# Attention scores of the later head pairs from 64x32 tiles over two banks, on queries without zeros

## The chip, the core and the metric

The kernel runs on one core of a Trainium2 chip. The core has TensorE (PE, whose weight loads are listed apart as PEld), VectorE (DVE), ScalarE (ACT), GpSimd (POOL) and SyncE (SP), which issues the DMA transfers here. The metric is the device time of one execution in microseconds (us), taken as the median of several runs. A profile is one further execution; it has a span (first to last instruction of the program) and a time of its own.

## The reference

Eight batches of eight heads, 576 positions, 64 dimensions per head. Heads 0 to 3 see the last 32 positions, heads 4 to 7 every fourth of the last 128. The result of attention goes through a gate with three matrices.

```python
scores = scale * np.matmul(q, k.transpose(0, 1, 3, 2))        # scale = 1/sqrt(64)
mask_plain = (rel >= 0) & (rel < window)                       # window = 32
mask_dil = (rel >= 0) & (rel < window * dilation) & (rel % dilation == 0)   # dilation = 4
scores = np.where(masks[None, :, :, :], scores, -1000000000.0)
attn = np.exp(scores - np.max(scores, axis=-1, keepdims=True))
attn = attn / (np.sum(attn, axis=-1, keepdims=True) + 1e-09)
x = np.matmul(attn, v)                                         # heads side by side: (8, 576, 512)
theta = x @ w_theta
zr, zi = x * np.cos(theta), x * np.sin(theta)
y = np.einsum('ts,bsd->btd', w_tok_r, zr) + np.einsum('ts,bsd->btd', w_tok_i, zi)
u = x + y
out = u + np.maximum(u @ w_ch, 0.0)
```

## The kernel before

**Attention.** The host sorts the positions of heads 4 to 7 by their remainder mod 4, so that each of their queries, too, needs only a band of keys. Heads go in pairs, four pairs in a batch (`NP = 4`), and queries in blocks of 32 (`QB`), 18 of them in a head (`2 * NJ`, `NJ = 9`). A block of 32 queries needs the 64 keys (`BW`) that end with its own. For a pair, the host lays the two heads' transposed queries one above the other on the 128 partitions, the 64 dimensions of the first on partitions 0 to 63 and those of the second on 64 to 127, and gives each block 64 columns: 32 for the first head with zeros on the lower half, 32 for the second with zeros on the upper half. One matmul with 128 rows and 64 columns of such a block (the weights) then streams 64 columns of keys and gives the scores of both heads (L614). Two blocks stand side by side in the partitions of a PSUM bank (`e` = 0, 1), five such double blocks in the pair's first bank `s`, four in its second. All are fp32; a profile has two records, and two weight loads, for each fp32 matmul.

**From scores to values.** VectorE adds the mask and takes the minimum into `P` and `mx` (L553), which frees the bank. ScalarE takes the exponentials (L649, three double blocks in one planned piece), VectorE their sums and reciprocals (L652, L653), GpSimd scales (L655). VectorE transposes 32x32 squares of `P` into `pt` in eight instructions (L673), and TensorE multiplies by the values (`o`, L773, 18 matmuls of 128 rows and 64 columns). ScalarE copies `o` out to `x` (L733) and rounds it to `xh` (L747), and the rest of `x` is taken by VectorE or GpSimd (L751, L753).

**The gate.** `th` (L842 to L849) is the product with `w_theta` in three fp32r matmuls of high and low parts each; the sine and cosine follow. In batches 0 and 1 the token product `y` (L1444) and in all batches the channel product `c` (L1477) are fp32r matmuls of 128x128 weights with 288 columns. From batch 2 on (`FIRST`) the token product is built from products `A`, `B`, `C` and `D` (L1235). VectorE adds `y` to `x` (L1418) and finishes `c` (L1453); ScalarE and GpSimd split sums into high and low parts (`u`: L481, L489, L1251, L1253).

**What sets the order.** All is recorded by a planner (`Order`): generators yield an engine and an estimated duration, and the planner lets the one with the lowest rank go first whose engine is free in its own reckoning. The instructions then stand in that order in each engine's queue. From the steady part on (`steady`), TensorE's order is written out by `phase`: while batch b goes through its token product, the scores of pairs 2 and 3 of batch b + 1 and of pairs 0 and 1 of batch b + 2 stand between its steps (`S_FAST`), and so do the value products of batch b + 1 (`PV_FAST`); the third figure that `phase` yields with each piece is the time for which it is entered in the plan, from which the ranks of the other engines' work (`due`) come. So a change of these figures moves rows of VectorE, ScalarE, GpSimd and SP, while TensorE keeps its order. Queries and keys are loaded two pairs ahead (`load_qk`, L322 and L324), values by `load_va` (L336).

## Time and profile before

| | |
|---|---|
| median of 3 runs | 557.34 us (555.86 to 557.61) |
| profiled execution | 555.45 us, span 553.7 us |
| granted clock of TensorE, mean | 0.994 |
| busy share: PE, PEld, DVE, ACT, POOL | 95%, 86%, 79%, 67%, 59% |
| scores of later pairs (L614, `s<-k,q`) | 1008 records in 28 pairs, 36.6 us busy |
| value products (L773, all) | 1152 records in 32 pairs |
| DMA | 124.42 MB, mean 225 GB/s |

The page gives busy time by engine, the span in 40 slices, the chain of work that ended last, the costliest groups of instructions and the DMA issues. In a row of a group or of the timeline, `s<-k,q 128*64 128x64 f32 x36` is a matmul that writes tile `s` from `k` and `q`, with weights of 128 rows and 64 columns, an output of 64 columns, and 36 records. A matmul's end is modelled; its start is measured. In the chain each piece begins where the piece ahead of it released it. A row of the view of waits has who waited, for whom, the sum in us, how often, and the longest.

### The profile page before, as it was taken

To read this page: it belongs to the slowest core of one execution; us is meant where nothing else is said; L and a number is where in the kernel's file an instruction comes from. 1 tells how busy PE (TensorE), PEld (TensorE's weight loads), DVE (VectorE), ACT (ScalarE), POOL (GpSimd) and SP (SyncE) were. 2 spreads that over 40 slices of the span, in tenths; PEclk is the share of its full clock that TensorE was granted. 3 is DMA by queue.
4 is the path that set the end of the run, shared out by engine and by line. 5 is a ranking of instruction groups with operands and counts; after the bars stand their busy time and mean duration, and the time that the engine had idled before them with its cause. 6 is when DMAs were issued, how large, how long until landed. Compare 5 with 4: busy or idle time off the path is not lost.

```text
span 553.7 us, 14354 instructions
## 1 busy us (share of the span) xinstructions
PE 528.7 (95%) x5296; PEld 478.8 (86%) x5296; DVE 435.5 (79%) x1359; ACT 373.1 (67%) x1029; POOL 329.4 (59%) x347
## 2 busy tenths in 40 slices
PE   5798898999999999999999999999999999999997
PEld 4643887888899899989999899989999899989997
DVE  3878897995588797989799988989799978848322
ACT  1589977858928478768775786768776777467320
POOL 1327868899774175655468375646468365817660
PEclk9999799999999999999999999999999999999999
DMA  8985245633578938994599828993698727680722
GB/s 297 400 332 186 99 139 202 222 144 119 165 256 265 343 155 283 341 282 173 189 326 306 299 86 274 363 281 118 236 325 282 277 90 219 209 274 28 233 85 86
DMA packets 59127, 124.42 MB, mean 225 GB/s; under 512 B 5424, under 2 KB 24624, under 8 KB 58800
## 3 DMA queue, kind: packets, MB, share of 16 engines
q1 hardware_dynamic: 59056, 123.49, 65.1%
q8 instruction: 42, 0.69, 0.5%
q14 instruction: 29, 0.24, 0.1%
HBM read 99.88 MB, written 23.59 MB: 223 GB/s over the span
## 4 chain that ended last, share of the span: by engine, by line
PE 65%; DVE 10%; DMA 9%; ACT 7%; POOL 5%; issue 2%; SPq 1%; POOLq 0%; ACTq 0%; DVEq 0%
PE c L1477 15%; PE th L842 11%; PE C L1235 8%; PE A L1235 7%; PE D L1235 6%; PE o L773 5%; PE B L1235 4%; PE s L614 4%; DVE pt L673 4%; DMA va<-in_vw_dram 3%; PE y L1444 2%; PE th L824 2%; DMA xn<-xd 1%; DMA st_wtk<-in_wtk_dram 1%; DMA q<-in_qT_dram 1%
## 5 line engine op out<-in xcount | busy, mean ns | idle before, releaser
L673 DVE STREAM_TRANSPOSE pt<-P 32x288 f32<-32x288 f32 x224 | 105.1, 469 | 13.1 <-POOL P L655 8.8
L1477 PE MATMUL c<-u,late_wc 128*128 128x288 f32 x768 | 109.1, 296 | 1.2 <-DVE x L1453 1.0
L1477 PEld LDWEIGHTS c<-u,late_wc 128*128 128x128 f32 x768 | 105.5, 188 | 4.7 <-DVE x L1453 1.5
L649 ACT ACTIVATE P<-P,mx 128x64 f32<-128x64 f32 x252 | 84.4, 337 | 2.9 <-DVE mx L553 2.6
L842 PE MATMUL th<-wthh,xh 128*128 128x512 f32 x224 | 75.0, 395 | 0.2 <-DVE K L1377 0.2
L655 POOL TENSOR_TENSOR P<-P,mx 128x576 f32<-128x576 f32 x32 | 38.2, 1192 | 57.6 <-DVE mx L653 50.4
L553 DVE CUSTOM_DVE_ANT_0 P<-s,mskb 128x64 f32<-128x64 f32 x252 | 39.0, 218 | 18.0 <-PE s L614 17.7
L1251 ACT CAST u<-x 128x288 fp32r<-128x288 f32 x48 | 20.6, 430 | 45.3 <-DVE x L1261 44.8
L842 PEld LDWEIGHTS th<-wthh,xh 128*128 128x128 f32 x224 | 42.0, 188 | 9.6 <-DVE K L1377 0.4
L1253 POOL TENSOR_TENSOR u<-x,u 128x288 fp32r<-128x288 f32 x48 | 41.6, 872 | 14.4 <-ACT u L1251 14.0
L649 ACT ACTIVATION_READ_ACCUMULATOR P<-P,mx 128x1 f32 x252 | 47.3, 188 | 0.0
L842 PE MATMUL th<-wthl,xh 128*128 128x512 f32 x112 | 44.4, 396 | 0.0
L733 ACT COPY x<-o 128x576 f32<-128x576 f32 x32 | 29.4, 920 | 19.6 <-PE o L773 19.5
L489 POOL TENSOR_TENSOR zl<-g,zh 128x512 fp32r<-128x512 f32 x7 | 9.1, 1298 | 53.5 <-ACT zh L481 53.5
L614 PE MATMUL s<-k,q 128*64 128x64 f32 x1008 | 36.6, 225 | 2.7 <-DVE K L1377 2.2
L614 PEld LDWEIGHTS s<-k,q 128*64 128x64 f32 x1008 | 32.8, 139 | 7.1 <-issue 2.7
L1453 DVE SCALAR_TENSOR_TENSOR x<-c,x 128x288 f32<-128x288 f32 x64 | 28.4, 451 | 11.6 <-PE c L1477 11.4
L773 PEld LDWEIGHTS o<-pt,va 128*64 128x64 f32 x600 | 20.4, 137 | 11.7 <-DVE pt L673 3.2
L773 PE MATMUL o<-pt,va 128*64 128x64 f32 x600 | 24.8, 227 | 5.8 <-DVE pt L673 2.9
L1015 POOL TENSOR_TENSOR s<-f,x 128x256 f32<-128x256 f32 x24 | 17.8, 740 | 12.2 <-DVE f L1003 10.0
L842 PEld LDWEIGHTS th<-wthl,xh 128*128 128x128 f32 x112 | 21.0, 188 | 4.2
L1095 POOL TENSOR_TENSOR s1l<-s,s1h 128x512 fp32r<-128x512 f32 x12 | 15.4, 1288 | 14.0 <-ACT s1h L1092 14.0
(232 smaller groups left out, 1576.3 us busy)
## 6 DMA issues: line engine op xcount, KB each, us to landing
q<-in_qT_dram SPq DMA_DIRECT2D x32, 576.0 KB, 6.0
late_wt_a<-tw_t SPq DMA_DIRECT2D x24, 576.0 KB, 6.8
wt_g<-tw_b SPq DMA_DIRECT2D x22, 576.0 KB, 6.4
va<-in_vw_dram SPq DMA_DIRECT2D x30, 320.0 KB, 4.9
k<-in_kT_dram SPq DMA_DIRECT2D x28, 304.0 KB, 6.2
out_dram<-x SPq DMA_DIRECT2D x28, 288.0 KB, 2.1
vb<-in_vw_dram SPq DMA_DIRECT2D x29, 256.0 KB, 4.5
xd<-xq SPq DMA_DIRECT2D x24, 288.0 KB, 5.3
```

The costliest lines, as they stand in the source:

```text
L553: pin(nc.vector.tensor_tensor_reduce(out=P[:, n], in0=ps[:, n - g0], in1=mskb[:, mask_of(pr, n)], op0=ALU.add, op1=ALU.min, scale=-SCALE, ...
L614: pe(nc.tensor.matmul(ps[64 * e:64 * e + 64, n - g0], q[:, qb], k[:, QB * qb:QB * qb + BW], start=not masked, stop=not masked or n == g1 - 1))
L649: table(nc.scalar.activation(P[:, n], P[:, n], AF.Exp, bias=mx[:, n:n + 1], scale=-1.0, accum_out=sm[:, n, :1]))
L655: pin(nc.gpsimd.tensor_tensor(P, P, mx.unsqueeze(2).to_broadcast([128, NJ, BW]), op=ALU.mult))
L673: pin(nc.vector.transpose(pmats[b, pr][k0:k0 + QB, :, hh, QB * e:QB * e + QB], P[p0:p0 + QB, :, QB * o:QB * o + QB]))
L733: pin(nc.scalar.copy(dst, src))
L773: pe(nc.tensor.matmul(ps[64 * hh:64 * hh + 64, BW * j:BW * j + BW], v[:, 64 * hh:64 * hh + 64], pmats[b, pr][:, j, hh], start=True, stop=T ...
L842: pe(nc.tensor.matmul(pt, l, r, start=(n == 0), stop=(n == 3 * NC - 1)))
L1235: pe(nc.tensor.matmul(ps, l, r, start=first and n == 1, stop=last and n == 3 * len(ks), skip_group_check=more))
L1253: pin(nc.gpsimd.tensor_tensor(ul[b, d][:, ts], x[:, ts], uh[b, d][:, ts].bitcast(F32), op=ALU.subtract))
L1453: pin(nc.vector.scalar_tensor_tensor(out=x[:, ts], in0=ps, scalar=0.0, in1=x[:, ts], op0=ALU.max, op1=ALU.add))
L1477: pe(nc.tensor.matmul(ps, l[:, cs], r[:, ts], start=(n == 0), stop=(n == 3 * NC - 1)))
```

## The change

It concerns the pairs from the third of batch 2 on (`EIGHT = 2 * NP + 2`, counted from 0: pairs 10 to 31, 22 of them). Their queries come without the zeros: 32 columns to a block, the first head on partitions 0 to 63 and the second on 64 to 127, half as many bytes. Each matmul of 128 rows and 64 columns becomes two of 64 rows and 32 columns, one for each head. There are eight places in the array for weights of this size, two by rows and four by columns, and the new function `eight` walks over all of them in turn: head 0's scores go to the first and third quarter of a bank's partitions and head 1's to the second and fourth, as before. For the first ten blocks, in the pair's first bank ("near"), head 0 stands on the lower 64 rows and head 1 on the upper; for the last eight, in the second bank ("far"), the host swaps the two heads' halves of `q` and `k` (`k` gets 32 more columns, since the two parts overlap). So the eight matmuls of four blocks, two near and two far, have eight different places, and no quarter of a bank is written from both row halves. `P`, the masks and everything behind are as before.

Also, `eight` takes both banks before its first matmul, and gives both to VectorE at its end, where each bank was taken and given by itself; the planner reckons 830 ns for a block (`SC_NS`) instead of 148 for each double block, and `phase` enters it for 0.85 instead of 1.35.

```diff
+JS = 5
+EIGHT = 2 * NP + 2
+KW = S + 32
...
+SC_NS = 830
...
         q = ap.tile([128, 2 * NJ, 2 * QB], F32, tag="q", name=f"q{b}_{pr}")
-        k = ap.tile([128, S + 32], F32, tag="k", name=f"k{b}_{pr}")
-        yield "DMA", dma(2 * S)
-        pin(nc.sync.dma_start(q, qT[b, pr]))
-        yield "DMA", dma(S + 32)
-        pin(nc.sync.dma_start(k, kT[b, pr]))
+        k = ap.tile([128, KW + QB], F32, tag="k", name=f"k{b}_{pr}")
+        if n < EIGHT:
+            yield "DMA", dma(2 * S)
+            pin(nc.sync.dma_start(q, q0[n]))
+        else:
+            q = q.rearrange("p a b -> p (a b)")[:, :S].rearrange("p (a b) -> p a b", b=QB)
+            yield "DMA", dma(S)
+            pin(nc.sync.dma_start(q, qT[n - EIGHT]))
+        w = KW if n < EIGHT else KW + QB
+        yield "DMA", dma(w)
+        pin(nc.sync.dma_start(k[:, :w], kT[b, pr][:, :w]))
...
+    def eight(b, pr, q, k, P, mx, held):
+        groups = ((0, JS), (JS, NJ))
+        for g0, g1 in groups:
+            ps, rel = yield from bank("s", f"s{b}_{pr}_{g0}")
+            held[g0] = ps[:, :(g1 - g0) * BW].rearrange("p (a b) -> p a b", b=BW), rel
+        yield "PE", SC_NS
+        for i in range(2 * NJ):
+            qb = i // 4 * 2 + i % 2 + 2 * JS * (i // 2 % 2)
+            if i >= 2 * 2 * (NJ - JS):
+                qb = 2 * JS - 2 + i % 2
+            n, e, far = qb // 2, qb % 2, int(qb >= 2 * JS)
+            for r in range(2):
+                rs, to = slice(64 * r, 64 * r + 64), QB * (2 * e + (1 - r if far else r))
+                pe(nc.tensor.matmul(held[JS * far][0][to:to + QB, n - JS * far], q[rs, qb],
+                                    k[rs, QB * (qb + far):QB * (qb + far) + BW], start=True, stop=True))
+        for g0, g1 in groups:
+            go(mask_scores(*held[g0], P, mx, pr, g0, g1, ("mask", b, pr, g0)))
...
-        for g0, g1 in ((0, 5), (5, NJ)):
+        if b * NP + pr >= EIGHT:
+            yield from eight(b, pr, q, k, P, mx, held)
+        for g0, g1 in ((0, 5), (5, NJ)) if not held else ():
...
-                        yield ("sc", c, q), scores(c, q), 1.35
+                        yield ("sc", c, q), scores(c, q), 1.35 if c * NP + q < EIGHT else .85
...
+    q0 = qT.reshape(B * NP, 128, 2 * NJ, 2 * QB)[:EIGHT]
+    near, far = 2 * JS, QB * 2 * JS
+    qh = qh.reshape(B * NP, 2, D, 2 * NJ, QB)[EIGHT:]
+    qT = np.concatenate([qh[:, :, :, :near], qh[:, ::-1, :, near:]], axis=3).reshape(-1, 128, 2 * NJ, QB)
+    kT = np.concatenate([kp[..., :far + QB], kp[:, ::-1, :, far:]], axis=3)
```

TensorE's order, in the first period that runs with `A` to `D`, at the scores of pair 3 of batch 3, behind the value product of pair 0. Before (`s_3_0` and `s_3_5` are the pair's two banks):

```order
L773 MATMUL o_0_2794<-pt_116,va_0_2154 64x64 x10
L773 MATMUL o_0_2794<-pt_116,vb_0_2267 64x64 x8
L614 MATMUL s_3_0_2815<-k_3_2297,q_3_2296 64x64 x10
L614 MATMUL s_3_5_2834<-k_3_2297,q_3_2296 64x64 x8
L1235 MATMUL B_0_2844<-wtkh_544,i1h_2460 128x288
```

Now:

```order
L803 MATMUL o_0_2880<-pt_116,va_0_2185 64x64 x10
L803 MATMUL o_0_2880<-pt_116,vb_0_2317 64x64 x8
L608 MATMUL s_3_0_2905<-k_3_2361,q_3_2360 32x64 x4
L608 MATMUL s_3_5_2906<-k_3_2361,q_3_2360 32x64 x4
L608 MATMUL s_3_0_2905<-k_3_2361,q_3_2360 32x64 x4
L608 MATMUL s_3_5_2906<-k_3_2361,q_3_2360 32x64 x4
L608 MATMUL s_3_0_2905<-k_3_2361,q_3_2360 32x64 x4
L608 MATMUL s_3_5_2906<-k_3_2361,q_3_2360 32x64 x4
L608 MATMUL s_3_0_2905<-k_3_2361,q_3_2360 32x64 x4
L608 MATMUL s_3_5_2906<-k_3_2361,q_3_2360 32x64 x4
L608 MATMUL s_3_0_2905<-k_3_2361,q_3_2360 32x64 x4
L1265 MATMUL B_0_2948<-wtkh_544,i1h_2528 128x288
```

The block stays where it was, with 36 matmuls for 18, four to one bank and four to the other in turn. No other row of TensorE moves.

VectorE's order in batch 1, while the `P` of batch 2's pairs 2 and 3 are transposed into `pt` and the last three `y` of the first half of the positions are added. Before:

```order
L753 TENSOR_TENSOR xh_0_1928<-x_0_1880,xh_0_1928 128x512
L673 STREAM_TRANSPOSE pt_116<-P_2_1798 32x9x32 x3
L1418 TENSOR_TENSOR x_1_1013<-y_1_0_1937,x_1_1013 128x288
L673 STREAM_TRANSPOSE pt_116<-P_2_1798 32x9x32
...
L478 CAST u_2_2079<-x_2_1188 128x288
L673 STREAM_TRANSPOSE pt_118<-P_3_1901 32x9x32 x4
L751 TENSOR_TENSOR xh_1_2036<-x_1_1997,xh_1_2036 128x64
L753 TENSOR_TENSOR xh_1_2036<-x_1_1997,xh_1_2036 128x512
L1418 TENSOR_TENSOR x_3_1342<-y_3_0_2078,x_3_1342 128x288
```

Now:

```order
L703 STREAM_TRANSPOSE pt_116<-P_2_1798 32x9x32
L1448 TENSOR_TENSOR x_1_1013<-y_1_0_1968,x_1_1013 128x288
L703 STREAM_TRANSPOSE pt_116<-P_2_1798 32x9x32 x3
...
L488 CAST u_2_2112<-x_2_1188 128x288
L703 STREAM_TRANSPOSE pt_118<-P_3_1918 32x9x32 x5
L1448 TENSOR_TENSOR x_3_1342<-y_3_0_2111,x_3_1342 128x288
L703 STREAM_TRANSPOSE pt_118<-P_3_1918 32x9x32
L783 TENSOR_TENSOR xh_0_1973<-x_0_1896,xh_0_1973 128x512
L781 TENSOR_TENSOR xh_1_2079<-x_1_2028,xh_1_2079 128x64
L783 TENSOR_TENSOR xh_1_2079<-x_1_2028,xh_1_2079 128x512
```

The sum with the fourth `y` (`y_3`) now stands ahead of the last transpose and of three `xh`, one of which stood ahead of all transposes.

SP's order in the same period as the first example, from the weights for `D` to the output of batch 2. Before:

```order
L1117 DMA wt_g<-tw_b_2489 128x1152 x2
L322 DMA q_2_3056<-in_qT_dram 128x1152
L324 DMA k_2_3057<-in_kT_dram 128x608
L336 DMA va_0_3025<-in_vw_dram 128x640
L354 DMA vb_0_3189<-in_vw_dram 128x512
L322 DMA q_3_3222<-in_qT_dram 128x1152
L908 DMA xd_3228<-xq_2851 32x18x128 x4
L1117 DMA wt_g<-tw_b_2468 128x1152 x2
L915 DMA xn_3334<-xd_3228 64x512
L915 DMA xn_3334<-xd_3228 128x512 x4
L324 DMA k_3_3223<-in_kT_dram 128x608
L336 DMA va_1_3188<-in_vw_dram 128x640
```

Now:

```order
L1147 DMA wt_g<-tw_b_2556 128x1152
L331 DMA q_2_3178<-in_qT_dram 128x576
L1147 DMA wt_g<-tw_b_2556 128x1152
L334 DMA k_2_3179<-in_kT_dram 128x640
L346 DMA va_0_3134<-in_vw_dram 128x640
L364 DMA vb_0_3316<-in_vw_dram 128x512
L346 DMA va_1_3315<-in_vw_dram 128x640
L938 DMA xd_3377<-xq_2951 32x18x128 x4
L1147 DMA wt_g<-tw_b_2533 128x1152 x2
L945 DMA xn_3459<-xd_3377 64x512
L945 DMA xn_3459<-xd_3377 128x512 x4
L331 DMA q_3_3359<-in_qT_dram 128x576
```

`va_1` moved ahead of `xd` and `xn`, `q_3` behind both, and the second half of the weights behind `q_2`.

More of the change, by code (lines that the diff above doesn't have):

```diff
@@ L249, in build @@
 @with_exitstack
-def build(ctx, tc, qT, kT, vw, wth, wtk, wch, maskb, ident, identb, outT):
+def build(ctx, tc, q0, qT, kT, vw, wth, wtk, wch, maskb, ident, identb, outT):
     nc = tc.nc
@@ L407, in first_loads @@
             yield "DMA", dma(2 * S)
-            pin(nc.sync.dma_start(q, qT[0, pr]))
+            pin(nc.sync.dma_start(q, q0[pr]))
             yield "DMA", dma(KE)
-            pin(nc.sync.dma_start(k, kT[0, pr]))
+            pin(nc.sync.dma_start(k, kT[0, pr][:, :KE]))
             qks[0, pr] = (q, k, None)
@@ L1667, in build @@
     steady()
-_INS = ["qT", "kT", "vw", "wth", "wtk", "wch", "maskb", "ident", "identb"]
+_INS = ["q0", "qT", "kT", "vw", "wth", "wtk", "wch", "maskb", "ident", "identb"]
 def _arrays(inp):
@@ L1687, in _arrays @@
         qT[:, :, hh, :, :, hh] = qh[:, :, hh]
-    qT = qT.reshape(B, NP, 128, 2 * NJ, 2 * QB)
-    kT = np.zeros((B, NP, 128, S + 32), k.dtype)
-    kT[..., 32:] = k.transpose(0, 1, 3, 2).reshape(B, NP, 128, S)
+    q0 = qT.reshape(B * NP, 128, 2 * NJ, 2 * QB)[:EIGHT]
+    kp = np.zeros((B * NP, 2, D, KW), k.dtype)
+    kp[..., 32:] = k.transpose(0, 1, 3, 2).reshape(B * NP, 2, D, S)
+    near, far = 2 * JS, QB * 2 * JS
+    qh = qh.reshape(B * NP, 2, D, 2 * NJ, QB)[EIGHT:]
+    qT = np.concatenate([qh[:, :, :, :near], qh[:, ::-1, :, near:]], axis=3).reshape(-1, 128, 2 * NJ, QB)
+    kT = np.concatenate([kp[..., :far + QB], kp[:, ::-1, :, far:]], axis=3)
+    kT[:EIGHT, ..., :KW] = kp[:EIGHT]
+    kT = kT.reshape(B, NP, 128, KW + QB)
     vp = np.zeros((B, H, S + 32, D), v.dtype)
@@ L1713, in _arrays @@
     identb = np.where(ident > 0, 0x3F80, 0).astype(np.uint16)
-    return dict(qT=qT, kT=kT, vw=vw, wth=wth, wtk=wtk, wch=wch, maskb=maskb, ident=ident, identb=identb)
+    return dict(q0=q0, qT=qT, kT=kT, vw=vw, wth=wth, wtk=wtk, wch=wch, maskb=maskb, ident=ident, identb=identb)
 def kernel(**inputs):
```

## The prediction

> **What bounds the kernel now.** I read the page's busy shares first, then the busy times by window of the repeating part, then the chain of waits in order of time, then who waited for whom on TensorE.
>
> ```profile
> span 553.7 us, 14354 instructions
> ...
> PE 528.7 (95%) x5296; PEld 478.8 (86%) x5296; DVE 435.5 (79%) x1359; ACT 373.1 (67%) x1029; POOL 329.4 (59%) x347
> ```
>
> TensorE is busy 95% of the span. An average says little, so the next view takes one of the periods in which a batch runs (there are four of them from 206 us on, each with four of the changed score blocks).
>
> ```profile
> core 0: us, PE busy (x) PEld busy (x) DVE busy (x) ACT busy (x) POOL busy (x), PEclk, DMA share, GB/s
> 206.00:267.40 61.40, 61.40 (x634) 57.49 (x636) 55.02 (x183) 45.47 (x136) 37.40 (x41) 1.00 0.76 256
> ```
>
> In this period of 61.40 us TensorE is busy for 61.40 at a granted clock of 1.00, and the next engine, VectorE, for 55.02. The chain of waits there is TensorE's own work, piece after piece (columns: start, length, what):
>
> ```profile
> 205.99 1.20 PE s L614 x36
> 207.19 2.58 PE A L1235 x18
> 209.77 1.20 PE o L773 x36
> 210.97 1.05 PE s L614 x36
> ```
>
> So a score block is on the path with its whole length: 36 records, two for each of its 18 fp32 matmuls. It takes 1.05 us when the value block `o` stands ahead of it, which uses the same tile shape, and 1.20 when a 128-row, 128-column matmul does. TensorE's waits from 120 us to the end are these, all of them:
>
> ```profile
> PE o L773 <- ACT x L733: 1.5, 1, 1.5
> PE c L1477 <- DVE x L1453: 1.0, 2, 0.8
> PE y L1444 <- DVE z L486: 0.2, 1, 0.2
> PE th L842 <- DVE K L1377: 0.2, 1, 0.2
> PE o L773 <- DMA vb<-in_vw_dram: 0.2, 1, 0.2
> ```
>
> The 1.5 us are one wait, at 166.82. By the timeline of TensorE three of the 22 changed blocks stand ahead of it (the first and the last below), and the fourth behind it:
>
> ```profile
> 138.36 1.27 PE L614 MATMUL s<-k,q 128*64 128x64 f32 x36
> 160.33 1.27 PE L614 MATMUL s<-k,q 128*64 128x64 f32 x35
> 168.06 1.22 PE L614 MATMUL s<-k,q 128*64 128x64 f32 x36
> ```
>
> Time saved in the three goes into that wait. The other 19 (this one, four in each of the four periods, two after them) save on the path: 5 of them come behind `c`, 14 behind `o`.
>
> **The score block itself.** How fast tiles run side by side is seen where two operands alternate, so that the merged timeline splits (columns: start, length, engine, line, what). Behind these rows stands one from the groups by line: the count, the busy us, the mean ns.
>
> ```profile
> 159.81 0.22 PE L773 MATMUL o<-pt,vb 128*64 128x64 f32 x1
> 159.86 0.22 PE L773 MATMUL o<-pt,va 128*64 128x64 f32 x1
> 159.87 0.34 PE L773 MATMUL o<-pt,vb 128*64 128x64 f32 x5
> L824 PE MATMUL th<-st_wth,x 128*128 128x512 f32 x32 | 16.5, 631 | 0.0
> ```
>
> Two records on the two column tiles start 0.01 us apart, and the next two 0.05 to 0.06 later: 1.05 us for 36 records is 18 steps of 0.0584, two tiles wide. What sets 0.0584? The fp32 matmuls with 512 columns take 16.5/32 = 0.516 us a record, 0.00101 a column, so 64 columns need 0.064: the step is the streaming of one tile's own 64 columns, not the cost of issuing. More tiles side by side therefore take no longer, as long as something else does not give out.
>
> The change makes each 128x64 matmul into two of 64 rows by 32 columns, over the same 64 streamed columns: 36 matmuls, 72 records, on eight tiles. By the order of the program the first 16 blocks of 32 queries give every tile four matmuls, and the last two give the four tiles of the near bank a fifth. The longest tile has 10 records: 10 x 0.0584 = **0.584 us** in place of 1.051, a saving of 0.467. I add 0.04 for the eight tiles' starts, which cannot all fall together (0.01 a start, half of it hidden at the end). Below 0.584 it can hardly go, since streaming sets it. Above, the nearest row is the present rate, one record in 0.0292: 72 x 0.0292 = 2.10 us. I take 0.584 + 0.04, by the two starts 0.01 apart, and keep the far end as a rival.
>
> **The switch of tile shape.** A block behind `o` now changes the shape, which it did not before. The chain prices it: 1.20 - 1.05 = 0.15 us. A second row, from the first batch, where 64x64 transposes and 128x64 scores follow each other:
>
> ```profile
> 15.67 0.68 PE L709 MATMUL pT<-ids,P 64*64 64x64 f32 x16
> 16.28 0.80 PE L614 MATMUL s<-first_k,q 128*64 128x64 f32 x20
> ```
>
> From 15.67 to 16.28 are 0.61 us for 16 records that need 8 x 0.0584 = 0.47: 0.14 for a switch between two small shapes. Between nothing (if 64x32 behind 128x64 needs no drain) and 0.15 I take **0.15** for each of the 14 blocks; the five behind `c` pay it already. Leaving the block costs the same as before, since what follows is 128x128 in both.
>
> Saved on the path: 5 x 0.467 + 14 x (0.467 - 0.15) - 19 x 0.04 = 2.34 + 4.44 - 0.76 = **6.0 us**.
>
> **The wait at 166.82.** The planner's new prices move rows of VectorE there. What holds TensorE is ScalarE's copy of `o` (L733), behind a cast of `u` (L481), behind VectorE's sum of the fourth `y` (L1418); the rows are those of the timelines of the three engines, one after the other:
>
> ```profile
> 154.40 1.43 DVE L673 STREAM_TRANSPOSE pt<-P 32x288 f32<-32x288 f32 x3 [4.08 <-POOL P L655]
> ...
> 162.06 1.93 DVE L673 STREAM_TRANSPOSE pt<-P 32x288 f32<-32x288 f32 x4
> 164.01 0.23 DVE L751 TENSOR_TENSOR xh<-x,xh 128x64 fp32r<-128x64 f32 x1
> 164.16 0.69 DVE L753 TENSOR_TENSOR xh<-x,xh 128x512 fp32r<-128x512 f32 x1
> 164.76 0.45 DVE L1418 TENSOR_TENSOR x<-y,x 128x288 f32<-128x288 f32 x1
> 165.24 0.43 ACT L481 CAST u<-x 128x288 fp32r<-128x288 f32 x1 [6.01 <-DVE x L1418]
> 165.58 1.19 ACT L733 COPY x<-o 128x576 f32<-128x576 f32 x1
> 165.07 0.29 PE L1444 MATMUL y<-late_wt_b,zl 128*128 128x288 f32 x1
> 166.82 0.80 PE L773 MATMUL o<-pt,va 128*64 128x64 f32 x20 [1.45 <-ACT x L733]
> ```
>
> The new order puts that sum ahead of the last transpose (0.48 us) and of both `xh` (164.01 to 164.76, 0.75), behind 15 of the 16 transposes: it runs some 1.2 us earlier. The first long `xh`, which ran in VectorE's idle time before 154.40, now comes after the sum and costs the path nothing. The last transpose then ends at about 164.4, before ScalarE's copy at 165.6, so the copy still decides. TensorE's own work ahead of it ends at 165.36 at the latest. Bounds: 0, if something else is late, to 1.45, the whole wait; I take **1.2**.
>
> **Edits at nothing.** A block now asks for both score banks before its first matmul. The tightest case is the block at 210.97: the masks of the block before it must have read both banks.
>
> ```profile
> 208.96 0.22 DVE L553 CUSTOM_DVE_ANT_0 P<-s,mskb 128x64 f32<-128x64 f32 x1
> ...
> 211.60 0.22 DVE L553 CUSTOM_DVE_ANT_0 P<-s,mskb 128x64 f32<-128x64 f32 x1 [2.41 <-PE s L614]
> ```
>
> The last mask ends at 209.18, and the block would start at 210.97 less the 0.5 or so saved ahead of it. That leaves over a microsecond; without this cover `B` and everything behind it on TensorE waits. The masks of the first half can start only when the whole block is done, but they started 211.60 - 210.97 = 0.63 us behind the block's start before, and the whole block now lasts about as long, so they come no later.
>
> ```profile
> q<-in_qT_dram SPq DMA_DIRECT2D x32, 576.0 KB, 6.0
> k<-in_kT_dram SPq DMA_DIRECT2D x28, 304.0 KB, 6.2
> 233.49 0.33 SPq L322 DMA_DIRECT2D q<-in_qT_dram  x1
> 272.38 1.05 PE s L614 x36
> ```
>
> The loads change from 576 and 304 KB to 288 and 320, so 272 KB less in each of 22 pairs, in as many issues. In SP's queue the fourth pair's `q` moves from ahead of `xd` and `xn` to behind both, a `va` takes its place, and half of a weight load now stands behind a `q`. That `q` was issued at 233.49 and its block starts at 272.38, 39 us later, against 6 to land. I count all of it as 0, bounds 0 to the 0.2 us that TensorE waits for `vb` above.
>
> **Sum.** 6.0 + 1.2 = 7.2 us. The profiled execution took 555.45 (span 553.7 and 1.75 around it) and would take 548.2; it lies 1.9 under the median of 557.34, so I forecast 557.34 - 7.2 = **550.1**.
>
> **The rivals.**
>
> *Row tiles don't run side by side.* If two tiles with different rows take turns, four are left, each with 18 records: 18 x 0.0584 = 1.05, as before, plus 14 x 0.15 = 2.1 for the switches, less 1.2: 557.34 + 0.9 = 558.2. For it: no row here shows two row tiles writing one bank at once; the 64x64 transposes use rows 0-63 and 64-127 on different columns and run in the same 0.0584 steps, which speaks against it. The Trainium skill, TensorEngine Tiling (Array Packing), "Gotcha 1: PSUM Pressure", says that different row tiles cannot access the same bank simultaneously; here both head halves write both banks, in different quarters of the partitions, and if the rule holds for a whole bank it gives this time.
>
> *Issue gives out* (the other side). Each record and its weight load needs a slot; if these cannot come faster than the 0.0292 us that any longer stretch of this trace shows, a block takes 2.10 us: 19 x 1.05 + 2.1 - 1.2 = +20.9, 578. It decides from (19 x 1.051 - 2.1 + 1.2)/(19 x 72) = 0.0139 us a record upward; below that the change gains. For it: twice the records, and no row with more than two tiles busy. Against it: pairs that start 0.01 apart, and steps that the streaming explains alone. The Trainium skill, TensorE: Matmul & The Clock Gate, "Wait — 56ns, not 53.3ns?", gives a smallest start-to-start of about 25 ns, which would make 72 x 0.025 = 1.8 us of a block and some 572 of the kernel. The pairs 0.01 us apart disagree with it between tiles, though not on the mean of 0.0292.
>
> *The gain is taken back.* TensorE gets 0.427 + 3 x 0.277 = 1.26 us ahead in each period; VectorE has 61.40 - 55.02 = 6.4 us of room, but its order is fixed, and a late transpose or `xh` would stop TensorE. Against it: the waits above are small at the present pace. If half of the 6.0 is lost, 553; if all, 556.
>
> **How the numbers follow.** Forecast 0.60, its own range 548 (no price for the switch) to 553 (blocks of 0.75 us); row tiles in turn 0.15; issue 0.12; taken back 0.13. A measurement of this kernel tells about 0.3% (1.7 us) from no change. Faster: 0.60 and most of the last case, 0.70. Within 0.3%: the rest of it and most of the row tiles, 0.13. Slower: 0.17. From 547 to 560 all but the issue case and the tails are held.
>
> **What would show it.** Score blocks of 72 records and 0.6 to 0.65 us on the chain behind `c`, 0.75 to 0.8 behind `o`; periods of about 60.1 us with TensorE busy throughout; the wait for ScalarE's copy under 0.5 us. Blocks of 1.05 show turns between row tiles, blocks of 1.5 or more the issue. The prediction is wrong if blocks are short and the periods are not.

## The result and the profile after

| | before | after |
|---|---|---|
| median | 557.14 us (555.45 to 558.35) | 553.24 us (552.33 to 555.84) |
| ratio | | 0.994, 95% interval 0.9917 to 0.9964 |
| profiled execution | 555.45 us, span 553.7 | 555.51 us, span 553.7 |
| block behind `o`, behind `c` (pieces of the chain) | 1.05, 1.20 us | 0.90, 0.90 us |

3.9 us came off, where 7.2 were forecast, and 553.24 lies beside the slow end, 553, of the forecast's own range. The profiled execution of the changed kernel is one of its slowest, 2.3 us above its own median, so its span says little and its stages say more.

These are rows of the page after: the span, the busy time, and the queue that fetches instructions (queue, kind: packets, MB, share).

```profile
span 553.7 us, 15941 instructions
...
PE 526.6 (95%) x6088; PEld 475.0 (86%) x6088; DVE 436.9 (79%) x1359; ACT 371.6 (67%) x1029; POOL 326.6 (59%) x347
...
q8 instruction: 48, 0.79, 0.6%
```

Before, the last of these rows was:

```profile
q8 instruction: 42, 0.69, 0.5%
```

TensorE has 792 matmul records and as many weight loads more (6088 for 5296). The program itself is fetched while it runs, on queue 8, in pieces of 16 KB (0.79 MB in 48), and six pieces more were fetched. This row has no part in the prediction; it comes back below.

The chain of waits after, at a block behind `c` and at one behind `o` (start, length, what):

```profile
269.99 1.06 PE c L1507 x8
271.05 0.90 PE s L608 x58
271.95 2.57 PE A L1265 x18
274.52 1.20 PE o L803 x36
275.72 0.90 PE s L608 x58
276.62 2.59 PE B L1265 x18
```

A block takes 0.90 us behind either: 0.30 less behind `c`, 0.15 less behind `o` (forecast 0.43 and 0.28). The busy time by window. The first row starts with `A` behind the first block of batch 3 and ends, as the prediction's row does, at 267.40, which is 4.7 us short of the period's end; the second is a whole period, from that `A` of one batch to that of the next:

```profile
core 0: us, PE busy (x) PEld busy (x) DVE busy (x) ACT busy (x) POOL busy (x), PEclk, DMA share, GB/s
206.12:267.40 61.28, 58.53 (x683) 54.03 (x679) 53.11 (x177) 44.18 (x133) 35.82 (x41) 0.97 0.71 231
272.06:332.72 60.66, 60.66 (x777) 56.45 (x778) 54.08 (x180) 43.88 (x133) 34.83 (x38) 1.00 0.71 234
```

From 272 on a period lasts 60.66 us instead of 61.40, with TensorE busy throughout: 0.30 + 3 x 0.15 = 0.75, all of it kept. Between 206 and 267 TensorE stands still for almost 3 us, and the whole first period, from 206.12 to 272.06, takes 65.94 us. The view of its waits from 120 us on tells where (its first five rows):

```profile
PE C L1265 <- DMA vb<-in_vw_dram: 2.5, 1, 2.5
PE s L608 <- DVE x L1483: 0.9, 1, 0.9
PE c L1507 <- DVE x L1483: 0.8, 1, 0.8
PE o L803 <- DMA vb<-in_vw_dram: 0.4, 2, 0.2
PE y L1474 <- ACT z L491: 0.4, 1, 0.4
```

The wait for ScalarE's copy, 1.5 us before, is gone. In its place stand two new ones, both in the first period that has changed blocks; TensorE's timeline has them here:

```profile
204.14 0.32 PE L608 MATMUL s<-k,q 64*32 64x64 f32 x8
205.33 0.86 PE L608 MATMUL s<-k,q 64*32 64x64 f32 x64 [0.88 <-DVE x L1483]
...
232.11 0.97 PE L608 MATMUL s<-k,q 64*32 64x64 f32 x72
235.56 0.82 PE L1265 MATMUL C<-late_wt_a,i2h 128*128 128x288 f32 x2 [2.48 <-DMA vb<-in_vw_dram]
```

At 204.14 the block's first eight records run, and then it waits for its second bank. At 232.9 TensorE stops for 2.5 us before a `C` that does not read `vb`, the transfer that the view names.

### The profile page after: what moved, and what is told of

It reads as the page before. It is cut to its first block, busy times and chain, and to the rows that moved or that the text cites. A ratio compares the mean times of both kernels' runs of the same rounds, so it can differ in the third digit from the quotient of the medians.

```text
span 553.7 us, 15941 instructions
## 1 busy us (share of the span) xinstructions
PE 526.6 (95%) x6088; PEld 475.0 (86%) x6088; DVE 436.9 (79%) x1359; ACT 371.6 (67%) x1029; POOL 326.6 (59%) x347
## 4 chain that ended last, share of the span: by engine, by line
PE 66%; DVE 11%; ACT 8%; POOL 6%; DMA 5%; issue 3%; SPq 1%; POOLq 0%; ACTq 0%; DVEq 0%
PE c L1507 14%; PE th L872 11%; PE C L1265 9%; PE D L1265 7%; PE A L1265 6%; PE o L803 5%; PE B L1265 4%; DVE pt L703 4%; PE s L608 3%; PE th L854 2%; POOL P L685 1%; DMA vb<-in_vw_dram 1%; DMA st_wch<-in_wch_dram 1%; DMA tw_t<-tx 1%; PE th L877 1%
## 5 line engine op out<-in xcount | busy, mean ns | idle before, releaser
L1283 POOL TENSOR_TENSOR u<-x,u 128x288 fp32r<-128x288 f32 x48 | 39.5, 827 | 17.6 <-ACT u L1281 17.4
L1013 ACT ACTIVATE cos<-f,halfpi 128x512 f32<-128x512 f32 (+1 forms) x30 | 20.7, 689 | 5.7 <-DVE g L952 5.5
L1265 PE MATMUL C<-late_wt_a,i2h 128*128 128x288 f32 x96 | 21.3, 315 | 2.5 <-DMA vb<-in_vw_dram 2.5
L608 PE MATMUL s<-k,q 64*32 64x64 f32 x1584 | 21.5, 224 | 0.9 <-DVE x L1483 0.9
```

The lines of the kernel that those rows point to most:

```text
L608: pe(nc.tensor.matmul(held[JS * far][0][to:to + QB, n - JS * far], q[rs, qb], k[rs, QB * (qb + far):QB * (qb + far) + BW], start=True, sto ...
L1265: pe(nc.tensor.matmul(ps, l, r, start=first and n == 1, stop=last and n == 3 * len(ks), skip_group_check=more))
L1283: pin(nc.gpsimd.tensor_tensor(ul[b, d][:, ts], x[:, ts], uh[b, d][:, ts].bitcast(F32), op=ALU.subtract))
```

## The experiments

The theories: (a) a block takes 0.90 because matmuls behind the first sixteen are supplied no faster than one in 0.0167 us; the rival is that the tiles themselves need so long. (b) The wait for the copy went with VectorE's new order; the rival is that the time comes back elsewhere. (c) The stop at 233 comes from the fetching of TensorE's instructions; the rival is a late transfer of data.

**The pace inside a block.** The starts of the records of the block at 275.65, in us from its first, taken from the trace one by one:

```
0.000 to 0.046   8 records, one each 0.0066     eight tiles
0.080 to 0.126   8
0.135 to 0.182   8
0.191 to 0.238   8                              sixteen matmuls so far
0.266, 0.322     the two of the seventeenth
0.330 to 0.597   a first record each 0.0167     17 matmuls
0.659, 0.676     the last two matmuls; the last record at 0.754
```

The first sixteen matmuls do what the forecast wanted of all: eight tiles run side by side, and a tile's records follow each other after 0.056 us. (Only its second record comes later, after 0.080.) Behind them the pace is one matmul in 0.0167 us, that is, a record in 0.0083, with a pause of some 0.046 twice.

*All matmuls of the 22 blocks issued twice:*

```diff
-        for i in range(2 * NJ):
+        for i in [i for _ in range(2) for i in range(2 * NJ)]:
```

> The 22 changed blocks with every matmul of the block issued a second time behind the first 36 (72 matmuls, 144 records). Theory one, streaming on eight tiles: 36/8 x 2 x 0.0584 = 0.526 us more, 1.28 from first to last start. Theory two, supply of matmuls at 0.0167 each with a pause of 0.046 after every seventeenth: 36 x 0.0167 + 2 x 0.046 = 0.69 more, 1.45, and the pauses show at the 17th, 34th, 51st and 68th matmul. A rate that falls off further (no more than one matmul in 0.03, as before the change) would give 1.8 or more.

An undisturbed block took 1.445 us from first to last start, where theory two gave 1.45. TensorE's timeline there, and the first row of its waits:

```profile
285.08 1.66 PE L608 MATMUL s<-k,q 64*32 64x64 f32 x144
286.67 0.40 PE L1265 MATMUL B<-wtkh,i1h 128*128 128x288 f32 x1
```

```profile
PE s L608 <- issue: 11.0, 6, 2.8
```

So theory two holds for the length; the pauses came, but not after every seventeenth matmul. The kernel took 587.2 us, ratio 1.0556 (1.0516 to 1.0596): 30 us more than before. Entry, block and exit together are 0.39 us longer behind `c` and 0.54 behind `o`, which explains 5 x 0.39 + 14 x 0.54 = 9.6. The view has 16.0 us in stops that neither an engine nor data released ("issue", of which the row shows 11.0), the first hint of what the stop at 233 is. Of the remaining 4 us some belong to four stretches of 3.4 us at half the granted clock from 240 us on, which the kernel before does not have.

*Four tiles at a time: the first bank's twenty matmuls, then the second's sixteen:*

```diff
-        for i in range(2 * NJ):
-            qb = i // 4 * 2 + i % 2 + 2 * JS * (i // 2 % 2)
...
+        for qb in range(2 * NJ):
```

> The 22 changed blocks with the same 36 matmuls in another order: the twenty of the first bank, then the sixteen of the second, so that four of the eight tiles work at a time. Theory one, four tiles stream in steps of 0.0584 us: (5 + 4) x 2 x 0.0584 = 1.05 us, as long as before the change, and no pause shows, since matmuls are wanted only every 0.029 us. Theory two, a tile needs 0.133 us for a matmul (0.078 from its first record to its second, 0.055 on to the next, as behind the sixteenth matmul now), whatever the supply: 9 x 0.133 = 1.20. If supply alone set the pace it would stay at 0.755. The kernel takes 19 x 0.3 = 5.6 us more than the changed one under theory one, less the wait for the second bank (0.7 to 1.0), which goes since that bank is needed 0.58 later.

```profile
336.81 1.11 PE L608 MATMUL s<-k,q 64*32 64x64 f32 x72
337.85 0.40 PE L1265 MATMUL B<-wtkh,i1h 128*128 128x288 f32 x1
```

0.89 us from first to last start, the figure of none of the theories. A tile's records came 0.056 apart, not 0.067 on the mean, so theory two falls; the total is under 1.05 because the second bank's matmuls began, at about 0.46, while the last of the first still ran, to about 0.55. Eight tiles beat four by 0.13 us a block, not by half. The kernel took 555.8 us, ratio 0.9976 (0.9949 to 1.0002).

*Streams half as long again, 96 columns for 64:*

```diff
-                pe(nc.tensor.matmul(held[JS * far][0][to:to + QB, n - JS * far], q[rs, qb],
-                                    k[rs, QB * (qb + far):QB * (qb + far) + BW], start=True, stop=True))
+                at, kc = BW * (n - JS * far), min(QB * (qb + far), KW - BW)
+                pe(nc.tensor.matmul(held[-JS * far - 1][to:to + QB, at:at + 96], q[rs, qb], k[rs, kc:kc + 96], start=True, stop=True))
```

> The 22 changed blocks with the same 36 matmuls in the same order, but each streams 96 key columns and not 64 (the 32 added columns are overwritten by the next double block; the last query block's scores are of keys 32 places earlier). With 64 columns a record on four tiles follows the one before on its tile after 0.056 us, so with 96 after 0.084. Theory one, supply at one matmul in 0.0167 us: a tile now needs 0.168 for a matmul and eight tiles one in 0.021, slower than the supply, so the tiles set the pace and the pauses are hidden: 9 x 0.084 + 0.046 = 0.80 us from first to last start, only 0.05 more than with 64 columns. Theory two, the tiles set the pace already with 64 columns (0.133 us a matmul and tile): the block grows with the columns, up to 0.754 x 1.5 = 1.13, and at least 0.754 + 10 x 0.028 = 1.03.

0.887 us: nearer to 0.80 than to 1.03, and the records say why it is neither. The first sixteen matmuls took 0.08 more (their records are now 0.083 apart on a tile, as expected), but the pace behind them was again one matmul in 0.0167, at 0.384, 0.400, 0.417, 0.434 and so on, although each streamed half as many columns again. So the pace of the second part is not the streaming. Nor is it the sharing of two banks by both row halves, since the first sixteen matmuls share them in the same way. Whether it is the issue of matmuls or of their weight loads, two records each, these runs don't tell apart, and a block with 32 columns was not measured.

**The planner's figures alone**, on the kernel before:

```diff
-            yield "PE", (148 if od.steady else 162) * (g1 - g0)
+            yield "PE", (830 / 9 if b * NP + pr >= 2 * NP + 2 else 148 if od.steady else 162) * (g1 - g0)
...
-                        yield ("sc", c, q), scores(c, q), 1.35
+                        yield ("sc", c, q), scores(c, q), 1.35 if c * NP + q < 2 * NP + 2 else .85
```

> The kernel before, with its own blocks of 36 records and its own loads, and only the planner's new figures (a score block reckoned at 0.83 and entered at 0.85). Theory one (the forecast's term of 1.2 us): TensorE's wait for ScalarE's copy near 166.8 goes from 1.45 to 0.2 or less, and the kernel takes 1.2 us less, about 555.9. Rival: the rows that move elsewhere make other waits, above all for VectorE's finish of c ahead of the first block of batch 3, and the time stays at 557.1 within 0.5.

TensorE's timeline at the place of the old wait, and at a new one:

```profile
166.29 0.29 PE L1444 MATMUL y<-late_wt_b,zl 128*128 128x288 f32 x1
166.52 0.80 PE L773 MATMUL o<-pt,va 128*64 128x64 f32 x20
...
197.39 0.47 PE L842 MATMUL th<-wthh,xh 128*128 128x512 f32 x1 [2.60 <-DVE g L922]
```

Where the wait of 1.45 stood, `o` follows `y` at once. But the ratio is 1.0037 (1.0015 to 1.0058), slower: a `th` now waits 2.6 us for VectorE, which itself stood 0.94 us for a load. VectorE's row, two ahead of the one that releases `th`:

```profile
195.50 0.68 DVE L922 TENSOR_TENSOR g<-xn,cos 64x512 f32<-64x512 f32 x1 [0.94 <-DMA xn<-xd]
```

Theory one was right about the place and wrong about the sum. The rival was right that other waits come, but not about where, and the time rose by 1.9 us instead of staying within 0.5. With the new blocks and their smaller loads this second wait is absent.

**The second bank.** The products `c` ahead of the block at 205 use the score banks for their fifth and sixth unit. VectorE's finish of the sixth, in the kernel before (first row) and in the changed one:

```profile
205.48 0.45 DVE L1453 SCALAR_TENSOR_TENSOR x<-c,x 128x288 f32<-128x288 f32 x1
204.82 0.45 DVE L1483 SCALAR_TENSOR_TENSOR x<-c,x 128x288 f32<-128x288 f32 x1
```

Before, it ended at 205.93, and the first matmul to the second bank came at 206.55, behind those to the first bank. Now it ends at 205.27, and that bank is wanted right behind the block's first four matmuls, whose last record starts at 204.24. Moving the units, in batches 1 and 2:

```diff
-            return (CHAN if b < B - 2 else CHAN6)[n - 2 * NC] if b < B - 1 else "mmx"[n % 3]
+            return (CHAN if 2 < b < B - 2 else "mmmssmxm" if b < B - 2 else CHAN6)[n - 2 * NC] if b < B - 1 else "mmx"[n % 3]
```

> The changed kernel, with the channel products c of batches 1 and 2 on other banks: the fourth and fifth of a batch take the two score banks (before: the fifth and sixth). No instruction moves. In two profiles the first block of batch 3 waited 1.0 and 0.7 us for its second bank, which VectorE's finish of the sixth c gave back. Theory one (that finish holds the block): the wait goes, the block there takes 0.755 us from first to last start and not 1.5 to 1.8, and the time falls by 0.7 to 1.0. Rival: VectorE is late there anyway, and the 0.7 to 1.0 come back as a wait a little later, at A, o or c.

In the waits of this kernel the row `s L608` is gone, and this one is new:

```profile
PE A L1265 <- DVE x L1483: 0.8, 1, 0.8
```

The block ran in 0.754 us, and `A` waited 0.8 at 207 for a later finish on VectorE. The ratio was 0.9936 (0.9915 to 0.9957), no different from the changed kernel's. A second assignment, with the sixth and seventh unit on `A`'s banks, is below (at the end of this chapter); there `A` waited 0.5 and the `o` behind it 0.4. So the theory was right about what held the block, and the rival about what it is worth: VectorE is late at 205 with all its rows, and the bank only decides which instruction of TensorE waits for it.

**The stop at 233.** First the changed kernel once more.

> The changed kernel once more, unchanged, for a second profile. In the first one TensorE waited 1.0 us inside the score block at 204.24 (for the second bank) and 2.6 us at 232.86 (before C), and the granted clock was 0.91 in the stretch 220 to 240. If these belong to the order of the program, both waits come back at the same two places; if the second is a chance of that execution, only the first comes back, the period from the first score block of batch 3 to that of batch 4 is about 62 us and not 66.8, and the time is about 552.5. Every score block should again take 0.754 us from its first to its last start.

Both waits came back, 0.6 and 1.9 us. The time was 555.13, ratio 0.9977 (0.9953 to 1.0001). A later set of runs of the same kernel on the same chip gave 0.9945 (below), so one such set leaves some 0.3% open. To see whether the stop has to do with instructions, I counted TensorE's records (weight loads, matmuls and its waits for semaphores) up to the start of each piece of program on queue 8. There is one piece for every 256 records. How many records behind its place a piece starts is its lateness, counted from the earliest piece of the same trace from 120 us on. In the kernel before, it was never more than 75 from 120 us on. Then I moved the places, by instructions that change nothing else: 32 (or 16) matmuls of the block at 139 issued twice.

```diff
-        for i in range(2 * NJ):
+        for i in [*range(16 * (b == 2 and pr == 2)), *range(2 * NJ)]:
```

> The changed kernel with the first 32 matmuls of the block of batch 2, pair 2 (at 139 us) issued twice: 128 more instructions for TensorE there (two weight loads and two matmuls each), all else the same. In two profiles TensorE stood still for 2.7 and 2.1 us at 232.9, with one of its instruction loads (16 KB, 256 instructions of TensorE between two of them) in flight, which began 236 to 267 instructions behind its place. Theory one, instructions: all later loads fall half a load earlier against the work, so the stop at 232.9 gets shorter than 0.5 us, or another one shows where the loads now fall badly; cost of the added matmuls at most 0.6 us, partly in TensorE's waits at 142 to 151. Theory two, data (a weight or value load on the DMA queues, which the order of SP sets): the stop at the same C stays at 2 to 2.7 us.

> As the one with 128 more instructions, but with 16 matmuls, 64 instructions. Theory one, instructions: loads fall a quarter of a load earlier against the work; the stop at 232.9 changes its length by 0.5 us or more, either way. Theory two, data: the stop stays at 2 to 2.7 us.

And by new blocks in two more pairs, in six more, and in one fewer (`EIGHT` 8, 4 and 11 for 10):

> The new blocks from the first pair of batch 2 on (24 in place of 22): 144 more instructions for TensorE ahead of 139 us, each of the two blocks 0.3 or 0.15 us shorter, in a stretch where TensorE is busy for 18 of 20 us. Theory one (stops come from where the instruction loads fall): 144 is about as far as the 128 that took the stop away, so no stop of over 1 us at the C behind the fourth block of batch 3's period, and the time is 551 to 552.5. Theory two (the stop came from the transfers at that place, and the copies of matmuls only changed the time at which TensorE comes there): the stop of about 2 us stays, 553 to 554.

> The new blocks from batch 1 on (28 in place of 22): 432 more instructions ahead of 139 us, 256 + 176. Theory one: the loads fall 176 instructions earlier against the work, further than in the two kernels that had no stop there, and I expect none of over 1 us at that C; the six added blocks stand where TensorE is not the only bound, so they bring 0 to 1 us: 550.5 to 552.5. Theory two: the stop stays, 552.5 to 554.

> The new blocks from the fourth pair of batch 2 on (21 in place of 22): 72 fewer instructions ahead of 139 us. Theory one: the loads fall 72 instructions later against the work, that is, 184 earlier than with the next load; where TensorE stood still for 2.1 to 2.7 us the load that was late by some 250 instructions is then wanted at another place, and the stop at that C is under 1 us or gone. The block of pair 2 costs 0.3 again. 552 to 553. Theory two: the stop stays, 553.5 to 554.5.

The profiles with the changed blocks, by the place of the pieces (records; lateness of the two pieces that start next to the stop or its place, and when; the stop). The two rows with other banks are of the kernels at the end of this chapter. The kernel with all matmuls twice is left out, since its places differ everywhere:

```
kernel                   moved   piece near 225   next piece      stop at the C near 233
the changed one           0      243 at 225.19    289 at 233.15   2.5
the same, again           0      248 at 225.54    236 at 232.82   1.9
the same, a third time    0      233 at 225.05     63 at 230.63   none
banks of c moved          0      247 at 225.43    170 at 232.25   1.7
four tiles at a time      0      254 at 225.80    232 at 232.81   1.7, inside the block
96 columns                0      245 at 225.10    291 at 232.90   2.3
16 matmuls more         +64       80 at 226.90    114 at 233.84   none
the same, again         +64      103 at 229.24    120 at 235.07   none
and banks, batch 2      +64       79 at 229.95    121 at 237.46   none
and banks, batch 1      +64       86 at 228.21    114 at 234.75   none
32 matmuls more        +128      134 at 228.77    169 at 235.67   none
24 new blocks          +144       51 at 224.74    135 at 232.59   none
28 new blocks          +432       63 at 223.18    175 at 232.05   none
21 new blocks           -72      173 at 226.37    227 at 234.62   none
```

At the original placing a piece is due at 220 to 222, just ahead of an `o` and a block of 144 records, and starts 3.5 to 5 us late; the next one is due at 226 and starts at 232 to 233 in the five profiles that stop. By then the next `o` and block have used up what was left: at the end of that block TensorE is 289 to 291 records past the place of a piece that is still being fetched, and stops. Where that piece began at 230.6, it did not stop. With the pieces moved it stops there in none of eight, though the order of SP's transfers in the kernels with 16 and 32 matmuls more is that of the changed kernel, row for row (the kernels with 24, 28 and 21 blocks have another). TensorE's timeline with 16 more, at the same time of the program:

```profile
232.45 0.97 PE L608 MATMUL s<-k,q 64*32 64x64 f32 x72
233.35 0.53 PE L1265 MATMUL C<-late_wt_a,i2h 128*128 128x288 f32 x2
```

The traces hold a sharper sign that needs no such zero. Number the pieces of a trace from 0, and count TensorE's records from its start. From 120 us on, fourteen stops of over 1 us (from one start to the next) are put down to "issue" or to a `vb` that the stopped matmul does not read: the five of the table, one at 423.3 in the kernel with 24 blocks, and eight in the kernel with all matmuls twice. In every one TensorE stands after exactly 256 k + 449 records while piece k is on its way, and goes on 1.2 to 1.6 us after it has come in. In the changed kernel piece 19 came in at 234.12, and TensorE went on at 235.45. In none of the 17 profiles, the kernel before among them, does a record beyond that count start earlier than 1.2 us after its piece has come in.

Theory (c) holds: TensorE stood at the end of the program that it had, and a transfer of data would not know of that place. `vb` was only what landed next. What makes a piece start late is not settled. The data queues are busy there (0.85 to 0.95 of the time between 220 and 240 us), but the 0.95 is that of the kernel before, whose pieces are at most 75 records late, and no kernel here took that load away.

The times of these kernels: 16 more 0.9916 (0.9897 to 0.9935) of the kernel before, 32 more 0.9964 (0.9947 to 0.9981), 21 blocks 0.9975 (0.9946 to 1.0004), a median of 554.9 us where 552 to 553 was expected. Those with 24 and 28 blocks missed what I expected by far, 1.0095 (1.0057 to 1.0133) and 1.0029 (1.0007 to 1.005): the orders of VectorE and SP changed in them, and that of TensorE ahead of 140 us. Their first rows of waits:

```profile
PE th L872 <- DVE g L952: 5.8, 1, 5.8
```

```profile
PE y L1474 <- DVE K L954: 3.0, 1, 3.0
PE y L1474 <- ACT late_wt_b L491: 2.1, 1, 2.1
```

The 24 blocks have the one stop elsewhere that is counted above, at 423.3 for 1.0 us in the view, beside a piece that started 275 records late.

**The two repairs together**, beside the changed kernel:

```diff
+        for i in [*range(8 * (b == 2 and pr == 2)), *range(2 * NJ)]:
...
+            return ("mmmssmmx" if b == 2 else CHAN if b < B - 2 else CHAN6)[n - 2 * NC] if b < B - 1 else "mmx"[n % 3]
```

> The changed kernel with 16 matmuls of the block of batch 2, pair 2 issued twice (64 more instructions for TensorE, which took the stop at 232.9 away and cost nothing, since TensorE waits just behind them) and, in batch 2, the channel products on banks so that the fourth and fifth hold the score banks, and the sixth and seventh the two banks of A. No instruction of another engine moves. Theory: no stop at 232.9 (2.1 to 2.7 us less than the changed kernel where that stops), the block at 205 without a wait (0.7 to 1.0 less), A in its place waits for the finish of the seventh c, which VectorE ends about 0.4 before that of the eighth, for which it waited 0.9: 0.5. Together 0.3 to 0.5 less than with the 64 instructions alone, 0.9 per cent below the kernel before. Rival: the other order of waits moves the instruction loads against the transfers again, and a stop comes back at another place; then it is no faster than 0.7 per cent.

> The changed kernel unchanged, beside the one with 64 more instructions and other banks, on the same chip. It should show the waits of its two profiles again, 0.7 to 1.0 us at 205 and 2 to 2.7 at 233, and take 2.5 to 3.5 us more than the other.

The ratio was 0.992 (0.9893 to 0.9948) against 0.9945 (0.9919 to 0.997) for the changed kernel, in whose third profile the stop was absent and the other wait was 0.4. Half a per cent (2.5 to 3.5 us) was expected between them, 0.9 us was measured, and the intervals don't separate them. The change of banks in batch 2 could not help: the `c` ahead of the block at 205 belong to batch 1, and the block waited 0.7 as ever. With `b == 1`:

> The changed kernel with 16 matmuls of the block of batch 2, pair 2 issued twice (64 more instructions) and, in batch 1, the channel products on banks so that the fourth and fifth hold the score banks, the sixth and seventh the two banks of A. No instruction of another engine moves. Theory: the block at 205 does not wait (0.4 to 1.0 us in the profiles so far); A waits instead for VectorE's finish of the seventh c, which in the profile of the kernel with the banks moved before ended some 0.4 us before that of the eighth, for which A waited 0.9, so A waits 0.5 or less: 0.2 to 0.5 less than with the 64 instructions alone. Rival: all of it comes back at A or o, and the time is that of the 64 instructions alone within 0.2.

> The kernel with the 64 added instructions alone once more, for more runs and beside the one with other banks. Theory: no stop at 233 in its profile, and 0.7 to 0.9 per cent below the kernel before. If the four runs so far were lucky, it comes to the 0.5 per cent of the changed kernel.

The ratio was 0.9938 (0.9916 to 0.9961) with the banks moved and 0.9934 (0.9909 to 0.9959) without, as the rival said. From the waits with the banks moved:

```profile
PE A L1265 <- DVE x L1483: 0.5, 1, 0.5
PE o L803 <- ACT s2h L1100: 0.4, 1, 0.4
```

No kernel here is shown to be faster than the changed one by more than the intervals leave open; the one with 16 more matmuls comes nearest.

## Why the prediction was wrong, and what of it was right

- **The path was right.** Periods without new waits shrank by what their four blocks lost: 61.40 - 60.66 = 0.74 against 0.30 + 3 x 0.15 = 0.75. Nothing was given back by VectorE's order there, though it is busy for 54 of 60.66 us. Two of the rivals fall with it: had row tiles taken turns, blocks had stayed at 1.05, and had issue been as slow as the bound taken, at 2.10. What the Trainium skill says in TensorEngine Tiling (Array Packing), "Gotcha 1: PSUM Pressure", that different row tiles cannot access one bank simultaneously, does not hold for a whole bank in this trace: both row halves wrote each bank with starts 0.0066 us apart. Nor does the smallest start-to-start of about 25 ns that the Trainium skill gives in TensorE: Matmul & The Clock Gate, "Wait — 56ns, not 53.3ns?", hold between tiles here: 0.0066 us in the first sixteen matmuls, 0.0083 a record behind them.
- **The size of a block was wrong, and this is the failed step**: "10 x 0.0584 = 0.584 us in place of 1.051", with the ground that the step is "not the cost of issuing. More tiles side by side therefore take no longer, as long as something else does not give out". Something did: behind the first sixteen matmuls TensorE was supplied with no more than one in 0.0167 us, whatever it streamed. From first to last start 9 x 0.0584 + 0.04 = 0.57 were forecast, 0.754 measured. The bound on the far side was worked out from the rate of two busy tiles (0.0292 a record). The whole block came to 0.754 / 71 = 0.0106 a record, below the point of 0.0139 from which it would have cost more than it brings, and so the sign held.
- **The switch of shape** was priced at 0.15 and cost 0.10 (last record of `o` to the first of the block 0.152 us, before 0.052). The difference of 1.20 and 1.05 from which it was read is not all switch: before, the block itself took 1.047 us from first to last start behind `c` and 0.998 behind `o`. In sum each block saves 0.13 less than forecast: measured, the blocks save 5 x 0.30 + 14 x 0.15 = 3.6 us on the path, where 6.0 were forecast.
- **The wait at 166.82** went as forecast, 1.45 of it where 1.2 were taken; the planner's figures alone did it too.
- **"Both score banks before its first matmul" at nothing was wrong.** The cover was shown for the block at 210.97, behind `o`; the block at 205 stands behind `c`, whose sixth unit holds the second bank until VectorE has finished it. Counted from the first block of batch 2, TensorE now comes there 1.5 to 2.1 us sooner, and it wants the second bank behind the block's first four matmuls, 0.10 us into the block, instead of at 0.63. It waits 0.4 to 0.9 us in the three profiles of the changed kernel.
- **Loads and SP's order at nothing** (bounds 0 to 0.2) was too little: `o` waits for `vb` 0.4 to 1.6 us in the three profiles, before 0.2.
- **The fetching of TensorE's own program was not thought of.** The stop took 0 to 2.5 us in one place, and in the first profile the slower clock behind it another 1.5. The forecast's own range ended at 553 for blocks of 0.75 us, and they were that (1.05 - 0.30), but that the time came out beside it is in part luck, since gains and losses that were not forecast partly cancel. The rival with half the gain taken back gave 553 too, and has the wait for VectorE at 205 in its favour; the rest is another mechanism.

Stage by stage, in the three profiles of the changed kernel, from the starts of the first block in each batch (TensorE's timeline; change against before, us):

| stage of the kernel before | forecast | first | second | third |
|---|---|---|---|---|
| 138.36 to 205.92 | -1.5 | -2.1 | -1.5 | -1.5 |
| 205.92 to 267.33 | -1.3 | +5.4 | +2.7 | +0.5 |
| 267.33 to 451.92, three periods | -3.8 | -2.6 | -2.6 | -1.6 |
| 451.92 to the end | -0.7 | -1.0 | -1.0 | -1.0 |
| sum | -7.2 | -0.3 | -2.4 | -3.6 |

The first stage came out as forecast in two of the three profiles. The last gained more than its two blocks explain (0.30 + 0.15): 0.5 come from a wait of TensorE for VectorE at 510, which is gone. The three periods lack the 0.13 of each block (and in the third profile 0.9 for a late `vb`). The second stage holds the bank and the stop, and in the first profile also 1.5 us at half the granted clock. The median of the timed executions, 3.9 less, lies with the third profile; how many of them had the stop is not known.

## What to carry to other kernels

Splitting a matmul for more tiles multiplies instructions: price the block by the supply of instructions as well as by the streaming, and find the supply from the fastest burst the trace shows beyond the first few records, not from a stretch that something else limits. Count how many instructions the denser code adds to TensorE's program and look at its fetches on the instruction queue; a stop that no data explains, and at which the engine always stands the same number of instructions past a piece still on its way, is one. Harmless instructions added far ahead move its place. When a block takes its buffers earlier, look up who holds them at every one of its places, not at the tightest one of the steady part.

## What was not expected of the hardware

- Eight tiles of 64 rows and 32 columns start records 0.0066 us apart, in runs of eight, for the first 32 records. Behind them a matmul of two records starts every 0.0167 us between pauses, whether it streams 64 or 96 columns.
- TensorE's program comes in pieces of 16 KB, one for 256 of its records, and a piece started up to 7.1 us behind its place in the changed kernel. In all fourteen stops TensorE stood after 256 k + 449 records while piece k was missing, and went on 1.2 to 1.6 us after it had come in.
- Behind the stop of 2.5 us the granted clock fell to half for 3.4 us (0.97 over the period), and the matmuls of `C` took 0.44 us for 0.29; behind that of 1.9 us it did not fall. The length of the stop alone does not decide it: with 96 columns the clock stayed at 1.00 behind a stop of 2.3 us, and with four tiles at a time it fell behind one of 1.7. What decides this stayed open.
